# Output stores moved behind block 3's transposing DMAs, the order inside block 0's second product, and block 4's first product as a plain one

## The chip, the core and the metric

The kernel runs on one core of a Trainium2 chip. The metric is the device time of one execution in microseconds (us). Engines are named as in the profile: PE is TensorE (PEld its weight loads), DVE is VectorE, ACT is ScalarE, POOL is GpSimd, SP is SyncE, which issues nearly all DMAs of this kernel.

## The reference, cut to what matters

```python
# retention: q, k, v of shape (B=4, H=8, S=768, D=64)
for t in range(S):
    state = gamma * state + k_t v_t^T           # one 64x64 state per batch and head
    y[:, :, t] = scale * q_t state
# the rows of y, heads side by side: x is (3072, 512)
h = x @ w_in                                    # (512, 2048)
g = h * tanh(softplus(h))                       # Mish
out = g @ w_out                                 # (2048, 512), float32
```

## The kernel before, in words

**Blocks.** The 3072 rows are 24 chunks of 128. Block 0 holds four chunks, each of the blocks 1 to 10 two; `first[blk]` is the first chunk of a block (0, 4, 6, 8, 10, 12 and so on). A block goes through retention (scores `at`, masked to `am`, outer products `u_ps`, states `mid` and `sth`, result `y_ps`, copied to `xt`), then the first product with `w_in` and Mish (`g`), then the second product with `w_out` (`o_ps`, collected in `osb`, stored to `out`). The parts of neighbouring blocks are interleaved by hand; every engine, SP's DMA queue among them, takes its instructions in the order in which the kernel writes them.

**The first product** has two forms. `g1(blk, u)` makes 64 plain matmuls of 128x256 for a block of two chunks (u = 0 to 7, eight matmuls each). `mixed_in(blk, last)` makes half of the product with seven smaller products in place of eight (Strassen-Winograd, 56 matmuls of 128x128, line 853) and half plain (32 of 128x256, line 873). Blocks from `MIX` on take `mixed_in`; in the kernel before `MIX` is 4. The sums of `mixed_in` go through six tiles of the tag `hsum`, asked for in this order: `m1` and `m5` (ACT copies, line 883), `h11` (DVE, line 888), `u2` (ACT), `h12` and `h22` (DVE). The last matmuls of `mixed_in`, `mm(pa, a(1, 1), t[3])`, write on the bank that `h22` reads.

**The second product** is `first_out` for block 0 and `seven(blk, ...)` for the others, both with seven products in place of eight. `seven` calls hooks between its products: `retain(blk + 1, later)` with `ready(later)`, which makes scores and outer products of the block after the next, and a hook that casts, transposes and loads what comes later.

**Chunks on their way in.** `load` issues three DMAs (q, k, v, lines 156 to 162). `casts_qk` (lines 422 and 425) and `casts_v` (line 432) scale and cast on POOL. `turn_by_dma` (line 437) transposes a chunk's q and k with one DMA into `qkt`. POOL's casts in `seven` begin with a one-column copy `summed` (line 1264), which reads a tile that DVE has just made, and so begin at a set point of the second product.

**Stores.** `seven` and `first_out` append the finished `osb` tiles to the list `stores`; `store_due(u)` (line 234) issues those that are due, inside the `g1` loop of blocks 1 to 3 and at the head of blocks from `MIX` on. `osb` has a tag of its own with five buffers. A pool hands out the buffers of a tag in the order in which they were given back; a tile that takes a buffer waits for the last reader of the tile before, and the last reader of an `osb` is its store.

**Helpers that the steps name.** `next_two(g)` runs in `seven(3)` with g = 14 and in `seven(4)` with g = 16: it transposes chunks g and g+1 and loads up to chunk g+3. `get_ready(blk + 1)` runs in the `g1` loop of blocks 1 to 3 (`tight`). In `first_out`, `turn_two` transposes chunks 4 and 5 on PE (line 255) and copies them out of PSUM with ACT and DVE; `kept_sum` makes `u3` on DVE (line 688); `outer_two` writes `u_ps` (line 353), which `pair_state` reads on DVE (line 366); `present_two` makes half of y (line 381) in two tiles of the tag `at`, which has two buffers, and `y_two` the rest.

Of the kernel before, what the change touches and what calls it, by code (L numbers as in the profile page):

```python
# [16 lines left out]
def kernel(  # L17
# [9 lines left out]
    nc = tc.nc  # L27
# [91 lines left out]
    loaded, cast, qkts, ats, ams, states, mids, us, ys = {}, {}, {}, {}, {}, {}, {}, {}, {}  # L119
    xts, gts, wins, wouts, wtmps = {}, {}, {}, {}, {}  # L120
    gtiles, tmats, gsums = {}, [], []
    ONE, MIX, BACK = 3, 4, 6
    nload, ncast = [0], [0]
    stores, weight_left, wsums = [], [], []

# [510 lines left out]
    def g1(blk, u):  # L636
        nt = BLOCKS[blk] * C
        per = TB // nt
        h_ps = g1_bank(blk, u)
        for j in range(per):  # L640
            s, f = divmod(u * per + j, FPS)
            for bp in range(NBP):
                wide = 2 * C if u >= NFB - 6 else nt
                for at in range(0, nt, wide):
                    cols = slice(at, at + wide)
                    nc.tensor.matmul(  # L646
                        h_ps[:, j, cols], wins[s][f // 2][:, bp, f % 2 * P:(f % 2 + 1) * P],
                        xts[blk][:, bp, cols], start=(bp == 0 and at == 0), stop=(bp == NBP - 1),
                        skip_group_check=blk == 0)
        room = NFB * TB // (2 * nt)  # L650
        at0, lies = divmod(u * per, room)
        if lies == 0:
            gtiles[blk, at0] = gp.tile([P, room, nt], FP16, name="g", tag="g", bufs=3)
        gt = gtiles[blk, at0][:, lies:lies + per]
        nc.scalar.activation(gt, h_ps, AF.Mish, scale=inv_boost3)  # L655
        for j in range(per):
            gts[blk, u * per + j] = gt[:, j]
# [33 lines left out]
    def first_out(load_more, cast_qk, cast_v, turn_two, sums, weight):  # L691

        hf = d_model // 2
        banks = {(0, 0): pxps.tile([P, 2, hf], FP32, name="o_ps", tag="px")}
        for ij in ((0, 1), (1, 0), (1, 1)):
            banks[ij] = mmps.tile([P, 2, hf], FP32, name="o_ps", tag="mm")
        open_banks = set(banks)
        osb = [op.tile([P, d_model], FP32, name="osb", tag="osb") for _ in range(CPB)]

        def mm(ij, x, w, fs=range(FPS)):  # L700
            for f in fs:
                for t in range(2):
                    nc.tensor.matmul(  # L703
                        banks[ij][:, t], x(f)[:, t * P:(t + 1) * P], w(f), start=ij in open_banks,
                        stop=f == fs[-1], skip_group_check=True)
                    open_banks.discard(ij)

        def a(i, j):
            return lambda f: gts[0, 2 * j * FPS + f][:, i * 2 * P:(i + 1) * 2 * P]

        def b(i, j):
            return lambda f: wouts[2 * i][:, f, j * hf:(j + 1) * hf]

        def s(i):
            return lambda f: sums[i - 1][:, f]

        def t(i):
            return lambda f: tmats[(i - 1) // 2][:, (i - 1) % 2, f]

        def plain(i, j, n, fs=range(FPS)):  # L720
            mm((i, j), lambda f: gts[0, n * FPS + f][:, i * 2 * P:(i + 1) * 2 * P],
               lambda f: wouts[n][:, f, j * hf:(j + 1) * hf], fs)

        def done(i, j, plus=None):
            for n in range(2):
                dst, src = osb[2 * i + n][:, j * hf:(j + 1) * hf], banks[i, j][:, n]
                if plus is None:
                    nc.scalar.copy(dst, src)
                else:
                    nc.vector.tensor_tensor(dst, src, plus[:, n], op=ALU.add)  # L730

        mm((0, 0), a(0, 0), b(0, 0))
        m1 = kept_sum(banks[0, 0])
        mm((0, 1), s(1), t(1))
        m5 = kept_sum(banks[0, 1])
        load_more()
        cast_qk()
        plain(1, 1, 1)
        plain(0, 0, 1)
        weight(0, 2)  # L740
        mm((0, 0), a(0, 1), b(1, 0))
        mm((0, 1), s(4), b(1, 1))
        mm((1, 0), s(2), t(2))
        u2 = kept_sum(banks[1, 0], m1)
        weight(0, 1)
        cast_v()
        turn_two()
        cast_wout(3, True)
        plain(0, 1, 1)
        mm((1, 0), s(3), t(3))  # L750
        u3 = kept_sum(banks[1, 0], m1)
        u35 = op.tile([P, 2, hf], FP32, name="hsum", tag="hsum", bufs=6)
        nc.gpsimd.tensor_tensor(u35, u3, m5, op=ALU.add)
        pair_scores(2, 0)
        pair_scores(2, 1)
        turn_both(CPB + 2)
        mm((1, 0), a(1, 1), t(4))
        plain(1, 0, 1)
        for j in (1, 0):
            plain(0, j, 3, range(2))  # L760
        outer_two()
        plain(0, 1, 3, range(2, FPS))
        done(0, 1, u2)
        plain(0, 0, 3, range(2, FPS))
        done(0, 0)
        present_two()
        weight(1, 1)
        plain(1, 0, 3)
        y_two()
        done(1, 0, m1)  # L770
        plain(1, 1, 3)
        done(1, 1, u35)
        for n in range(CPB):
            stores.append((0, out_rows(0, n), osb[n]))
# [150 lines left out]
    def seven(blk, masks, hooks, last):  # L925
        n, hf = NFB // 2, d_model // 2
        px = pxps.tile([P, hf], FP32, name="o_ps", tag="px")
        pb = mmps.tile([P, hf], FP32, name="o_ps", tag="mm")
        osb = [op.tile([P, d_model], FP32, name="osb", tag="osb") for _ in range(2)]

        def a(i, j):
            return lambda f: gts[blk, j * n + f][:, i * P:(i + 1) * P]
# [261 lines left out]
    def outer_two():  # L1194
        u = u_banks()[1][:1]
        for a in range(2):
            pair_outer(2, u, a)
        pair_state(2, u, 0)
# [7 lines left out]
    def y_two():  # L1206
        y = pairs["y"]
        pair_present(2, y, True)
        for m in range(2):
            pair_past(2, y, m)  # L1210
        for m in range(2):
            pair_xt(2, y, m, m == 1)
# [15 lines left out]
    def next_chunk(g):  # L1228
        turn_next(g)
        load_to(g + 3)  # L1230

    def next_two(g):
        turn_next(g)
        load_to(g + 3)
        turn_next(g + 1)
        load_to(g + 4)

    def next_one(g):
# [22 lines left out]
    def cast_behind(blk, i):  # L1261
        g = first[blk] + (6 if blk == 1 else 8)
        if ncast[0] < min(g, NCK):
            nc.gpsimd.tensor_copy(summed, gsums[blk % 2][:, i, NFB // 2 - 1, P - 1:])  # L1264
            if blk == 1:
                for n in range(g - 2, g):
                    casts_qk(n)
                for n in range(g - 2, g):
                    casts_v(n)
                ncast[0] = g  # L1270
            elif blk + 1 >= BACK:
                cast_to(g - 2)
                casts_qk(g - 2)
                ncast[0] = g
            else:
                cast_to(min(g, nload[0]))

    def tight(blk):

# [1 line left out]

    def plan_of(blk):
        a = first[blk] + 4
        plan = {u: [] for u in (0, 1, 5)}
        if tight(blk):
            plan[5] = [(get_ready, blk + 1)]
        elif blk < MIX:
            plan[0] = [(settle, blk + 1), (mask_two, blk + 1), (leave, blk + 1)]
        if blk == 1:
            plan[0] += [(load_to, a + 2)]  # L1290
            plan[1] += [(begin_load, a + 2)]
        elif blk < ONE:
            plan[1] += [(next_chunk, a)]
        return plan

    first_block()
    for blk in range(1, len(BLOCKS)):
        last = blk + 1 == len(BLOCKS)
        plan = plan_of(blk)
        if blk >= BACK:  # L1300
            second_of(blk - 1)
        if blk >= MIX:
            store_due(NFB)
            mixed_in(blk, last)
        elif blk > 1:
            weight_left.extend(in_sums(blk - 2))
        for u in range(NFB // 2 if blk < MIX else 0):
            store_due(u)
            g1(blk, u)
            if u in ((6, 7) if tight(blk) else (5, 7)):  # L1310
                sums_a(blk, u // 7)
            for fn, *args in plan.get(u, ()):
                fn(*args)
            if weight_left:
                weight_left.pop(0)()
        hooks = [[], [], []]
        if not last:
            later = blk + 2 if ONE <= blk < len(BLOCKS) - 2 else None
            hooks = [[(retain, blk + 1, later)],
                     [(next_one, first[blk] + 6)] if blk + 1 >= BACK else  # L1320
                     [(next_two, first[blk] + 6)] if blk >= ONE else
                     [(turn_load, first[blk] + 4)] if blk == 1 else
                     [(next_chunk, first[blk] + 5), (turn_load, first[blk] + 6)],
                     [(finish, blk + 1)] if later is None else []]
        if tight(blk):
            hooks[2].append((leave, blk + 1))
        seven(blk, [(mask_two, blk + 1)] if tight(blk) else [], hooks, last)
# [31 lines left out]
```

## Time and profile before

| what | value |
|---|---|
| device time, median of 3 runs | 197.19 us (196.53, 197.19, 197.45) |
| the profiled execution | 196.68 us, its span 194.9 us |
| mean granted TensorE clock | 0.998 |
| PE busy | 188.6 us (97%), 3124 matmuls |
| DVE, ACT, POOL busy | 138.8 (71%), 104.4 (54%), 74.5 us (38%) |
| DMA | 38.78 MB, mean 199 GB/s |

Times inside the text are counted from the start of the span. "x8" is a count of instructions, "[0.59 <-DMA ...]" the idle time of the engine before a row and what ended it. A DMA's row shows how long SP was held by issuing it; its landing is later.

### The profile page before, as it was taken

Reading aid. Unit: us, or ns where it says so; the run is one execution under the profiler, and the core shown is the slowest. Engines: PE = TensorE matmul, PEld = TensorE weight load, DVE = VectorE, ACT = ScalarE, POOL = GpSimd, SP = SyncE. Lnnn points to the kernel's source line nnn. Section 1 sums busy time; section 2 is a strip of 40 time slices with the busy share of each in tenths; the row PEclk is TensorE's granted clock in tenths of the full one; section 3 lists DMA queues with packets and bytes.
Section 4 is the critical chain, followed back from the end, with each engine's and each line's share of the span. In section 5 each row is a group of like instructions: output and inputs, shape, how many; then the busy total and the mean of one; then the engine's idle time right before and its main releaser. Section 6 shows DMA issues by size and latency. Waiting matters only on the chain.

```text
span 194.9 us, 7190 instructions
## 1 busy us (share of the span) xinstructions
PE 188.6 (97%) x3124; PEld 162.1 (83%) x3124; DVE 138.8 (71%) x270; ACT 104.4 (54%) x194; POOL 74.5 (38%) x98
## 2 busy tenths in 40 slices
PE   7998999899999999999998999999999999999993
PEld 7756478787888888888997998998998988988993
DVE  0796559875867877967983985965885885885462
ACT  3375766244552552554483584484574763763850
POOL 5362000578507846662647605525625700000000
PEclk9999999999999999999999999999999999999999
DMA  5999999999999999999999999999895250300202
GB/s 173 304 310 348 367 385 364 289 306 215 131 257 261 177 236 213 206 194 194 247 233 197 227 182 290 202 213 255 98 241 106 52 148 3 111 0 26 89 29 81
DMA packets 84303, 38.78 MB, mean 199 GB/s; under 512 B 57776, under 2 KB 78896, under 8 KB 84272
## 3 DMA queue, kind: packets, MB, share of 16 engines
q1 hardware_dynamic: 84128, 38.28, 87.4%
q8 instruction: 24, 0.39, 0.9%
q10 hardware_dynamic: 144, 0.05, 0.2%
q14 instruction: 7, 0.06, 0.1%
HBM read 27.31 MB, written 6.29 MB: 172 GB/s over the span
## 4 chain that ended last, share of the span: by engine, by line
PE 51%; DMA 25%; SPq 12%; POOL 6%; DVE 2%; issue 1%; ACT 1%; POOLq 0%
PE o_ps L946 21%; PE h_ps L873 11%; DMA qf<-in_q_dram 10%; PE h_ps L853 10%; DMA vf<-in_v_dram 5%; DMA wi<-in_moe_w_in_dram 5%; SPq L284 4%; SPq L188 3%; PE o_ps L703 3%; DMA qkt<-qk 3%; PE h_ps L646 3%; SPq L162 2%; POOL v L432 2%; DMA kf<-in_k_dram 2%; SPq L437 2%; PE y_ps L559 2%
## 5 line engine op out<-in xcount | busy, mean ns | idle before, releaser
L646 PE MATMUL h_ps<-xt,win 128*128 128x256 f16 (+1 forms) x272 | 34.3, 285 | 0.0
L946 PEld LDWEIGHTS <-gsum 128*128 128x128 f16 x320 | 30.3, 98 | 3.8
L646 PEld LDWEIGHTS <-win 128*128 128x128 f16 x272 | 26.3, 98 | 6.6
L655 ACT ACTIVATE g<-h_ps 128x512 f16<-128x512 f32 x38 | 22.7, 597 | 15.2 <-PE h_ps L646 15.2
L946 PE MATMUL o_ps<-tmat,gsum 128*128 128x256 f16 x240 | 29.7, 273 | 0.0
L873 PE MATMUL h_ps<-xt,win 128*128 128x256 f16 x224 | 29.0, 273 | 0.0
L946 PEld LDWEIGHTS <-g 128*128 128x128 f16 x248 | 23.4, 98 | 2.6
L961 DVE TENSOR_TENSOR osb<-o_ps,snap 128x256 f32<-128x256 f32 (+1 forms) x33 | 13.8, 417 | 13.5 <-PE o_ps L946 9.6
L952 ACT COPY snap<-o_ps 128x256 f32<-128x256 f32 (+1 forms) x33 | 12.2, 369 | 20.1 <-PE o_ps L946 20.1
L873 PEld LDWEIGHTS <-win 128*128 128x128 f16 x224 | 20.7, 98 | 1.9
L864 ACT ACTIVATE g<-h_ps 128x512 f16<-128x512 f32 x35 | 19.9, 587 | 3.1 <-PE h_ps L873 3.1
L422 POOL TENSOR_TENSOR qk<-qf,qvs 128x512 f16<-128x512 f32 x18 | 19.4, 1076 | 4.3 <-DMA qf<-in_q_dram 4.3
L432 POOL TENSOR_TENSOR v<-vf,qvs 128x512 f16<-128x512 f32 x18 | 19.5, 1093 | 2.8 <-DMA vf<-in_v_dram 2.7
L883 ACT COPY hsum<-h_ps 128x512 f32<-128x512 f32 x21 | 12.3, 585 | 15.1 <-PE h_ps L853 14.9
L425 POOL TENSOR_TENSOR qk<-kf,qvs 128x512 f16<-128x512 f32 x18 | 18.8, 1042 | 4.2 <-DMA kf<-in_k_dram 4.0
L888 DVE TENSOR_TENSOR hsum<-h_ps,hsum 128x512 f32<-128x512 f32 x21 | 14.5, 691 | 7.4 <-PE h_ps L853 5.2
L946 PE MATMUL o_ps<-wout,g 128*128 128x256 f16 x160 | 19.1, 273 | 0.0
L608 ACT CAST xt<-y_ps 128x512 f16<-128x512 f32 x15 | 10.2, 735 | 11.1 <-PE y_ps L559 11.1
L853 PE MATMUL h_ps<-xt,wsum 128*128 128x128 f16 x224 | 15.9, 219 | 0.0
L1264 POOL COPY summed<-gsum 128x1 f16<-128x1 f16 x7 | 3.0, 422 | 33.3 <-DVE gsum L813 27.0
L853 PEld LDWEIGHTS <-wsum 128*128 128x128 f16 x224 | 14.0, 98 | 0.3
L864 ACT ACTIVATE g<-hsum 128x512 f16<-128x512 f32 x21 | 13.3, 631 | 1.5 <-DVE hsum L888 1.4
(112 smaller groups left out, 301.6 us busy)
## 6 DMA issues: line engine op xcount, KB each, us to landing
kf<-in_k_dram SPq DMA_DIRECT2D x24, 256.0 KB, 5.2
vf<-in_v_dram SPq DMA_DIRECT2D x24, 256.0 KB, 5.6
out_dram<-osb SPq DMA_DIRECT2D x22, 256.0 KB, 3.8
qf<-in_q_dram SPq DMA_DIRECT2D x20, 256.0 KB, 4.6
wi<-in_moe_w_in_dram SPq DMA_DIRECT2D x6, 512.0 KB, 8.8
wt<-in_moe_w_out_dram SPq DMA_DIRECT2D x2, 1024.0 KB, 10.3
wt<-in_moe_w_out_dram SPq DMA_DIRECT2D x4, 512.0 KB, 7.9
qfirst<-in_q_dram SPq DMA_DIRECT2D x2, 512.0 KB, 4.6
```

What stands on the lines that cost most here:

```text
L422: nc.gpsimd.tensor_tensor(in_place(q16.rearrange("p (w x) d -> p w x d", x=2)), by_head(qf), scale_by_head(qs_two[:, heads]), op=ALU.mult)
L425: nc.gpsimd.tensor_tensor(k16.rearrange("p (y w) d -> p w y d", y=2), kf.rearrange("p (w y) d -> p w y d", y=2), boosts.rearrange("p (w y) ...
L432: nc.gpsimd.tensor_tensor(cast[g][2], loaded.pop(g)[2], vs[g % 2].unsqueeze(2).broadcast_to((P, H, D)), op=ALU.mult)
L646: nc.tensor.matmul(h_ps[:, j, cols], wins[s][f // 2][:, bp, f % 2 * P:(f % 2 + 1) * P], xts[blk][:, bp, cols], start=(bp == 0 and at == 0) ...
L655: nc.scalar.activation(gt, h_ps, AF.Mish, scale=inv_boost3)
L853: nc.tensor.matmul(o_ps[:, f], w(f // 2, k)[:, f % 2 * P:(f % 2 + 1) * P], x[:, k], start=begin and f == 0 and k == 0, stop=k == 1, skip_g ...
L864: nc.scalar.activation(to, src, AF.Mish, scale=inv_boost3)
L873: nc.tensor.matmul(h_ps[:, f], wins[w][h // 2][:, k, h % 2 * P:(h % 2 + 1) * P], xts[blk][:, k, :2 * C], start=k == 0, stop=k == NBP - 1)
L883: nc.scalar.copy(m, o_ps)
L888: nc.vector.tensor_tensor(m, x, y, op=ALU.add)
L946: nc.tensor.matmul(o_ps[:, cols], x(f), w(f)[:, cols], start=first and z == 0, stop=z == n - 1, skip_group_check=True)
L961: nc.vector.tensor_tensor(dst, o_ps[:, cols], plus, op=ALU.add)
```

## The change: what it does

The stores leave the `g1` loop. `store(n)` issues the next n of the list: four (block 0's) in `next_two(14)`, behind the transposing DMAs of chunks 14 and 15 and around the loads of chunk 16; two (block 1's) at the head of block 4; four (block 2's and block 3's) in `next_two(16)`: two ahead of the transposing DMA of chunk 17, two behind the loads of chunk 18. As more of them are unstored at a time, the `osb` tiles of blocks 1 to 3 come from the tag `hsum`. `MIX` becomes 5, so block 4's first product is plain. In `first_out` eight plain matmuls go ahead of `turn_two`, `present_two` goes right behind `outer_two` with `y_two` earlier too, and one DVE sum moves into block 1. Block 1's `get_ready` goes one u later. POOL's casts of blocks 2 to 4 take q and k of both chunks first, then v. In block 0, u = 5 to 9 are made in columns of 256 instead of 512.

```diff
-    ONE, MIX, BACK = 3, 4, 6
+    ONE, MIX, BACK = 3, 5, 6
...
-                wide = 2 * C if u >= NFB - 6 else nt
+                wide = 2 * C if u >= 5 else nt
...
         cast_v()
+        plain(0, 1, 1)
         turn_two()
         cast_wout(3, True)
-        plain(0, 1, 1)
         mm((1, 0), s(3), t(3))
...
         outer_two()
+        present_two()
+        plain(1, 0, 3, range(2))
         plain(0, 1, 3, range(2, FPS))
         done(0, 1, u2)
         plain(0, 0, 3, range(2, FPS))
         done(0, 0)
-        present_two()
-        weight(1, 1)
-        plain(1, 0, 3)
         y_two()
+        weight(1, 0)
+        plain(1, 0, 3, range(2, FPS))
         done(1, 0, m1)
...
-        osb = [op.tile([P, d_model], FP32, name="osb", tag="osb") for _ in range(2)]
+        osb = [
+            op.tile([P, d_model], FP32, name="osb", tag="osb") if blk > ONE else
+            op.tile([P, d_model], FP32, name="osb", tag="hsum", bufs=6) for _ in range(2)]
...
+    def store(n):
+        for _ in range(n):
+            _, dst, osb = stores.pop(0)
+            nc.sync.dma_start(dst, osb)
+
     def next_two(g):
         turn_next(g)
-        load_to(g + 3)
-        turn_next(g + 1)
+        if g == first[ONE] + 6:
+            turn_next(g + 1)
+            store(2)
+            load_to(g + 3)
+        else:
+            store(2)
+            turn_next(g + 1)
+            load_to(g + 3)
+        store(2)
         load_to(g + 4)
...
-                cast_to(min(g, nload[0]))
+                both = range(ncast[0], min(g, nload[0]))
+                for n in both:
+                    casts_qk(n)
+                for n in both:
+                    casts_v(n)
+                ncast[0] = both.stop
...
-        plan = {u: [] for u in (0, 1, 5)}
+        ready_at = 6 if blk == 1 else 5
+        plan = {u: [] for u in (0, 1, ready_at)}
         if tight(blk):
-            plan[5] = [(get_ready, blk + 1)]
+            plan[ready_at] = [(get_ready, blk + 1)]
...
-        elif blk > 1:
+        elif blk in (2, 3):
             weight_left.extend(in_sums(blk - 2))
+        elif blk == MIX - 1:
+            store(2)
         for u in range(NFB // 2 if blk < MIX else 0):
-            store_due(u)
             g1(blk, u)
```

## The prediction

> **What bounds the kernel now.** I read the page first: PE is busy for 188.6 of 194.9 us, so what counts is PE's order and its few idle moments. I then asked for PE's own waits:
>
> ```profile
> PE at L480 <- DMA qkt<-qk: 0.6, 1, 0.6
> PE t_ps L255 <- POOL qk L305: 0.5, 1, 0.5
> PE o_ps L703 <- DVE hsum L688: 0.2, 1, 0.2
> ```
>
> From 16 us to the last matmul at 191.9 these are nearly all. The first is the one place where a DMA reaches PE: at 105.57, in block 4's second product, the transposed chunk 15. The chain of waits runs through that DMA back along SP, POOL's casts and the loads to 55.8, so the DMA queue has run just in time for 50 us. The stages of blocks 4 and 5, and the end:
>
> ```profile
> 93.78:108.64 14.86, 14.27 (x267) 12.86 (x264) 11.15 (x27) 8.64 (x16) 8.55 (x9) 1.00 1.08 226
> 108.64:122.95 14.31, 14.31 (x269) 13.02 (x267) 10.72 (x25) 8.51 (x16) 4.58 (x5) 1.00 1.25 234
> 192.00:194.90 2.90, 0.00 (x0) 0.00 (x0) 0.27 (x1) 0.00 (x0) 0.00 (x0) 0.88 0.32 102
> ```
>
> The columns are length, busy PE, PEld, DVE, ACT, POOL, granted clock, DMA share, GB/s. The DMA engines are full (1.08 and 1.25) in both stages. SP's timeline shows the queue pushing back; a transposing DMA's issue takes 1.24 at 149.38, when the queue is empty, and 3.68 here:
>
> ```profile
> 105.39 1.69 SPq L234 DMA_DIRECT2D out_dram<-osb  x2
> 107.18 2.21 SPq L437 DMA_TRANSPOSE qkt<-qk  x1
> 109.45 0.58 SPq L162 DMA_DIRECT2D qf<-in_q_dram  x1
> 110.08 0.53 SPq L162 DMA_DIRECT2D kf<-in_k_dram  x1
> 110.65 1.20 SPq L162 DMA_DIRECT2D vf<-in_v_dram  x1
> 111.96 3.68 SPq L437 DMA_TRANSPOSE qkt<-qk  x1
> ```
>
> These are block 3's stores, chunk 16's transpose, chunk 18's loads and chunk 17's transpose. The last lands 6.0 after its issue, at 117.9 (the tile's own view at that time).
>
> **Small parts on PE.**
>
> *Block 4's plain first product.* It removes 56 matmuls of 128x128 and 32 of 128x256 (6.69 us, 93.78 to 100.47) and adds 64 of 128x256. Blocks 2 and 3 run these at 0.1094 each (line 646, 48 in 5.25): 7.00. **+0.31**. The sums that go (seven DVE, three ACT) were beside PE; block 5's mask and states move into 7 us of `g1`, where DVE has room.
>
> *Columns of 256.* 20 matmuls of 512 (0.2158 start to start) become 40 of 256 (0.1092): **+0.05**.
>
> *Chunk 15's transpose.* Eight stores (blocks 0 to 2) that were issued before it go behind it; each takes the queue about 0.65 (two of 256 KB land 5.5 and 4.9 after issues 1.31 apart). It comes some 5 us earlier; the wait goes: **-0.59**. Next late on PE there is nothing else.
>
> *`first_out`.* The eight matmuls fill the 0.5 before `turn_two`, but all turns now run behind them and end 0.2 later (four of them ran before the wait). From there the chain is ACT's two copies (1.08), DVE's two (0.76) and `u3` (0.61), which PE awaited for 0.2 already; what was filled ahead is waited for there, and PE resumes 0.2 later than before. Then `present_two` comes right behind `outer_two`. Its second tile takes the buffer that DVE's `mid` reads:
>
> ```profile
> 45.26 0.42 DVE L366 TENSOR_TENSOR mid<-u_ps,sth 128x256 f16<-128x256 f32 x1 [0.98 <-PE u_ps L353]
> ```
>
> ```profile
> 44.78 0.44 PE L353 MATMUL u_ps<-v,qk 64*64 64x64 f16 x16
> 45.15 1.05 PE L703 MATMUL o_ps<-wout,g 128*128 128x256 f16 x8
> 46.13 0.25 PE L381 MATMUL y_ps<-am,v 64*64 64x128 f16 x4
> ```
>
> Eight matmuls from 45.15 to 46.13 covered `mid`, over at 45.68. Without them PE waits about 0.5. One change of matmul shape fewer gives back 0.1. **+0.6** (ends 0.2 and 0.9).
>
> *At nothing:* the DVE sum that moves (0.68) falls into DVE's idle 1.98 ahead of 54.79; `get_ready` one u later delays three states of 0.42, read 5 us later; POOL's new order brings the second k 1.04 sooner, and v, later by 2.1, is read after the transpose has landed. Uncovered, each costs its own length, all under 2.1.
>
> So PE comes to block 5's last product of `mixed_in` at 114.88 + 0.31 + 0.05 - 0.59 + 0.6 = 115.25.
>
> **The part that decides: `hsum`.** After the change all six `hsum` buffers hold the unstored `osb` of blocks 1 to 3. Block 5's `mixed_in` asks for six again; in the order of return `m1`, `m5` take block 1's, `h11`, `u2` block 2's, and **`h12`, `h22` block 3's**, whose stores are issued behind the transpose of chunk 17 and the loads of chunk 18. DVE takes its instructions in order: `h12` waits, and behind it `h22`, the states and the sums of `g`; PE then waits at `mm(pa, a(1, 1), t[3])` for `h22`. Before, block 5 ran:
>
> ```profile
> 112.00 0.69 DVE L888 TENSOR_TENSOR hsum<-h_ps,hsum 128x512 f32<-128x512 f32 x1
> 113.04 0.69 DVE L888 TENSOR_TENSOR hsum<-h_ps,hsum 128x512 f32<-128x512 f32 x1 [0.36 <-ACT hsum L883]
> 114.14 0.69 DVE L888 TENSOR_TENSOR hsum<-h_ps,hsum 128x512 f32<-128x512 f32 x1 [0.40 <-PE h_ps L853]
> ```
>
> ```profile
> 114.88 0.61 PE L853 MATMUL h_ps<-xt,win 128*128 128x128 f16 x8
> ```
>
> *When do the stores land?* Up to block 3's second store the new order has on SP just what the old one has up to chunk 17's transpose: ten stores, loads to chunk 18, transposes to 17. A full queue that works in order ends the same set at the same time: 117.9. It is later by what the queue idles. The transpose of chunk 14 can't be issued before its k is cast, which begins at a point of block 3's second product (cast over at 93.6, or 94.2 with PE 0.6 later), while the loads ahead, rid of six stores, land near 98.1 - 3.9 = 94.2: with the transpose's 3.1 from an empty queue, about 2 idle. I take 1 of the 2: 118.9. Block 1's and block 2's stores, a transpose and more ahead, land by about 113 and hold up little.
>
> *Then:* the first store is 0.65 ahead, `h12` 0.69, `h22` 0.69 behind the second, PE at 118.9 + 0.9 = 119.8. PE waits **4.55** (3.55 without idle queue, 5.55 with all of it). ACT has five Mish of 0.6 queued behind `h12`, which `seven(5)` reads: **+0.4** (0 to 0.6).
>
> *The clock.* Two rows show what idleness does: the first 46 matmuls of 128x128 take 5.09 us (107 ns each; 56 in block 5), and at the end the clock falls (0.88 over 2.9 us with PE at 0: a half for the last 0.7, so 2.2 us after the last matmul). A 4.5 us wait is longer than 2.2: the clock halves, and up to 5.1 us then run at half speed, which loses 0 to 2.55. I take **+1.5**. The Trainium skill (TensorE: Matmul & The Clock Gate, The HAM clock gate) states that the clock halves after a whole idle window of about 3.4 us, the windows running freely; by that a wait of 4.55 would hold a whole one in only a third of the cases. The row at the end, 2.2 us, speaks for less, and I go by the row.
>
> **Sum**, against the profiled execution's own 196.68 (1.78 outside its span; 0.51 below the median 197.19, so a median may come 0.5 higher): +0.37 by 115.25, +4.55, +0.4, +1.5 = +6.8: **203.5 us**.
>
> **Rivals.**
>
> *A: the queue keeps its lead, and PE never waits (not slower).* 196.68 + 0.37 = 197.05. It decides at the second store's landing: by 115.25 - 0.9 = 114.35. For it: in an empty queue k of 16 cast at 107, transposes issued in 1.24 each, stores in 0.4, loads in 0.6 and a landing of 2.3 (155.73) give about 114.8, close to the point. Against: shares of 1.08 and 1.25 and issues held 3.68; eight more stores lie in just this stretch. The same time comes if `h12` were not to take block 3's buffer, so that the change in `hsum` isn't what I read. 8%.
>
> *B: as A, and `first_out` gains.* If `mid` doesn't hold `present_two`, and both waits there (0.7) go: 196.68 + 0.36 - 0.59 - 0.7 = 195.75, over 0.5% faster by a hair. Against: the chain ACT, DVE, `u3` is untouched. 5%.
>
> *C: the wait is there, the clock stays.* 203.5 - 1.5 = 202.0 (a wait within whole windows, or shorter). With the stores at 116.5, if part of the lead is kept, 196.68 + 0.37 + 2.15 + 0.2 = 199.4. 27%.
>
> *D: forecast* with its bounds: 60%, from 201 (wait 3.55, clock 0.4) to 206.4 (wait 5.55, ACT 0.6, clock 2.55, and 0.6 more if `first_out` and queue are both at their worst).
>
> **Numbers.** 0.5% is 1.0 us, about what this measurement can tell from no change. Faster by more: B, 0.05. Within: A, 0.08. Slower: C and D, 0.87. The range runs from C's lower case, 199.4, to D's upper end, 206.4; outside lie A and B and little else.
>
> **What would show it.** In the changed profile: PE's longest wait is `h_ps` L853 on DVE `hsum` L888, 3.5 to 6 us, near 115 to 120; DVE's L888 waits there for DMA `out_dram<-osb`; the clock is below 1.00 in that slice or the next. PE `at` L480 no longer waits for `qkt`; PE L381 waits for DVE L366 near 45.5; block 1 starts 0.6 later; block 4's L646 takes 7.0. I am wrong if block 3's stores land before 114.3, or if `h12` starts without them.

## The result: 5.3% slower, by a wait that the prediction names and sizes too small, and by the clock behind it

The changed kernel takes 207.82 us (median of 207.43, 207.60, 207.82, 207.98 and 208.37; a sixth execution, disturbed, took 486.44 us and is left out), the kernel before 197.38 (median of 6). The ratio is 1.0531, 95% interval 1.0498 to 1.0564. The profiled execution took 207.82 us, its span 205.9 us, against 196.68 and 194.9: +11.1 where +6.8 was forecast: the direction is right, the size is outside the range (199.4 to 206.4 us).

PE's own waits in the changed kernel, the three longest behind the start of the program (total, times, longest; us):

```profile
PE h_ps L854 <- DVE hsum L889: 3.9, 1, 3.9
PE h_ps L854 <- ACT g L865: 2.4, 1, 2.4
...
PE y_ps L381 <- DVE mid L366: 0.5, 1, 0.5
```

The first and the third are as forecast (line 888 is now 889, 853 is 854); the second, and the size of what hangs on both, are not. The wait for `qkt` at L480 is gone. Block 5 in PE's timeline:

```profile
113.96 0.61 PE L854 MATMUL h_ps<-xt,win 128*128 128x128 f16 x8 [2.40 <-ACT g L865]
...
115.48 1.92 PE L874 MATMUL h_ps<-xt,win 128*128 128x256 f16 x8
...
123.22 1.01 PE L854 MATMUL h_ps<-xt,win 128*128 128x128 f16 x8 [3.91 <-DVE hsum L889]
```

Before, the last of these rows stood at 114.88 and took 0.61; eight matmuls of 128x256 took 1.04, not 1.92. So there are two waits, and half speed behind each. (A row of PE lasts to the modelled end of its last matmul; from start to start the eight of 128x256 took 1.71, before 0.87, and the eight of 128x128 0.81, before 0.45.) Who was waited for, in ACT's and then in DVE's timeline:

```profile
112.83 0.58 ACT L884 COPY hsum<-h_ps 128x512 f32<-128x512 f32 x1 [5.21 <-DMA out_dram<-osb]
```

```profile
121.88 1.29 DVE L889 TENSOR_TENSOR hsum<-h_ps,hsum 128x512 f32<-128x512 f32 x2 [6.15 <-DMA out_dram<-osb]
```

Both end on stores: `m1` on block 1's (landed 112.75), `h12` and `h22` on block 3's (landed 121.75 and 122.44). Block 1's were issued from 106.73 on, ahead of chunk 16's transpose. SP's timeline shows block 2's just ahead of chunk 17's transpose and block 3's behind it and the loads of chunk 18; this last pair held SP for 3.09:

```profile
111.72 1.08 SPq L1238 DMA_DIRECT2D out_dram<-osb  x2
112.91 1.44 SPq L437 DMA_TRANSPOSE qkt<-qk  x1
...
116.34 3.09 SPq L1238 DMA_DIRECT2D out_dram<-osb  x2
```

The windows of two us in and behind the first wait, and of block 5's `mixed_in` and `seven` (length, busy PE, PEld, DVE, ACT, POOL, granted clock, DMA share, GB/s):

```profile
112.00:114.00 2.00, 0.04 (x1) 0.03 (x1) 0.17 (x1) 1.17 (x3) 2.00 (x3) 1.00 1.22 185
...
116.00:118.00 2.00, 2.00 (x15) 1.63 (x14) 0.00 (x0) 0.79 (x2) 0.00 (x0) 0.50 1.02 243
...
108.76:124.03 15.27, 8.96 (x91) 7.77 (x89) 5.88 (x12) 4.61 (x9) 4.08 (x4) 0.82 1.10 263
124.03:133.79 9.76, 9.76 (x178) 7.77 (x177) 4.67 (x12) 3.62 (x8) 2.51 (x3) 0.76 0.69 161
```

The clock's records are at a half from 115.09 to 118.50 and from 121.92 to 128.74. Before, `mixed_in(5)` took 6.69 (now 15.27) and `seven(5)` 7.45 (now 9.76). From block 6 on the two executions run alike, the changed one 11.0 later. So the whole loss is block 5:

| step, at PE | forecast | measured |
|---|---|---|
| start of block 5 | +0.37 | +0.12 (108.76, before 108.64) |
| wait at the last product of `mixed_in(5)` | +4.55 | +8.22 (123.22 less 114.88 + 0.12) |
| that product and `seven(5)`: clock and ACT | +1.9 | +2.67 (0.81 - 0.45, 9.76 - 7.45) |
| start of block 6 | +6.82 | +11.01 |

### The profile page after: what moved, and what is told of

The parts are those of the page before. It is cut to its first block, busy times and chain, and to the rows that moved or that the text cites. A ratio compares the mean times of both kernels' runs of the same rounds, so it can differ in the third digit from the quotient of the medians.

```text
span 205.9 us, 7172 instructions
## 1 busy us (share of the span) xinstructions
PE 193.2 (94%) x3120; PEld 166.5 (81%) x3120; DVE 133.3 (65%) x263; ACT 102.5 (50%) x191; POOL 73.3 (36%) x98
## 4 chain that ended last, share of the span: by engine, by line
PE 82%; DMA 8%; DVE 2%; SPq 2%; ACT 1%; issue 1%; POOL 1%; DVEq 0%
PE o_ps L949 29%; PE h_ps L646 20%; PE h_ps L874 8%; PE h_ps L854 8%; PE o_ps L703 6%; DMA kf<-in_k_dram 3%; DMA out_dram<-osb 3%; PE y_ps L559 3%; DMA qfirst<-in_q_dram 2%; PE t_ps L255 1%; PE u_ps L487 1%; PE at L480 1%; SPq L162 1%; PE y_ps L381 1%; PE h_ps L628 1%
## 5 line engine op out<-in xcount | busy, mean ns | idle before, releaser
L646 PE MATMUL h_ps<-xt,win 128*128 128x256 f16 (+1 forms) x356 | 41.5, 276 | 0.0
L646 PEld LDWEIGHTS <-win 128*128 128x128 f16 x356 | 34.6, 98 | 5.4
L655 ACT ACTIVATE g<-h_ps 128x512 f16<-128x512 f32 x46 | 27.5, 597 | 19.8 <-PE h_ps L646 19.8
L949 PEld LDWEIGHTS <-g 128*128 128x128 f16 x248 | 24.2, 101 | 3.4
L874 PE MATMUL h_ps<-xt,win 128*128 128x256 f16 x192 | 26.0, 280 | 0.0
L889 DVE TENSOR_TENSOR hsum<-h_ps,hsum 128x512 f32<-128x512 f32 x18 | 12.4, 691 | 15.2 <-PE h_ps L854 7.0
L949 PE MATMUL o_ps<-wout,g 128*128 128x256 f16 x160 | 20.8, 287 | 0.0
L874 PEld LDWEIGHTS <-win 128*128 128x128 f16 x192 | 18.4, 101 | 2.0
L884 ACT COPY hsum<-h_ps 128x512 f32<-128x512 f32 x18 | 10.5, 586 | 16.6 <-PE h_ps L854 10.6
L865 ACT ACTIVATE g<-h_ps 128x512 f16<-128x512 f32 x30 | 17.1, 590 | 2.4 <-PE h_ps L874 2.4
L854 PE MATMUL h_ps<-xt,win 128*128 128x128 f16 x144 | 11.4, 224 | 6.3 <-DVE hsum L889 3.9
L854 PEld LDWEIGHTS <-win 128*128 128x128 f16 x144 | 9.8, 100 | 7.4 <-issue 6.7
L865 ACT ACTIVATE g<-hsum 128x512 f16<-128x512 f32 x18 | 11.3, 630 | 7.2 <-DVE hsum L889 7.2
```

The lines of the kernel that those rows point to most:

```text
L646: nc.tensor.matmul(h_ps[:, j, cols], wins[s][f // 2][:, bp, f % 2 * P:(f % 2 + 1) * P], xts[blk][:, bp, cols], start=(bp == 0 and at == 0) ...
L854: nc.tensor.matmul(o_ps[:, f], w(f // 2, k)[:, f % 2 * P:(f % 2 + 1) * P], x[:, k], start=begin and f == 0 and k == 0, stop=k == 1, skip_g ...
L865: nc.scalar.activation(to, src, AF.Mish, scale=inv_boost3)
L874: nc.tensor.matmul(h_ps[:, f], wins[w][h // 2][:, k, h % 2 * P:(h % 2 + 1) * P], xts[blk][:, k, :2 * C], start=k == 0, stop=k == NBP - 1)
L889: nc.vector.tensor_tensor(m, x, y, op=ALU.add)
L949: nc.tensor.matmul(o_ps[:, cols], x(f), w(f)[:, cols], start=first and z == 0, stop=z == n - 1, skip_group_check=True)
```

## Experiments

The theory: the shared tag `hsum` makes block 5's sums wait for late stores, and the clock falls in the waits. Rivals: the stores' new places by themselves (through late loads and transposes), block 4's plain product, and the order in block 0. All ratios are against the kernel before, run beside on the same chip.

**Nobody asks for the six tiles** (x_mix6).

```diff
-    ONE, MIX, BACK = 3, 5, 6
+    ONE, MIX, BACK = 3, 6, 6
...
-        elif blk == MIX - 1:
+        elif blk == 4:
             store(2)
+        elif blk == 5:
+            store_due(NFB)
```

> The changed kernel with MIX 6: block 5's first product is plain too, so that nothing asks for the six hsum tiles before block 6; the DMA order is kept (block 1's stores at the head of block 4, block 4's at the head of block 5). Theory (hsum: block 5's sums wait for buffers whose stores land at 112.8 to 122.4): PE has no wait over 0.5 us between 100 and 130, the granted clock stays full, and the time is that of the kernel before, 197.4, plus 0.54 (block 0) - 0.72 (block 4's second product) + 0.30 (block 4) + 0.3 (block 5's plain product): 197.8. Rival (the stores' new place itself, through late loads and transposes, whatever holds the buffers): 203 or more, with PE or the casts waiting for DMAs behind block 5.

197.72 us against 197.51, ratio 1.0019 (0.9998 to 1.0039): the 5% are gone with every store still at its new place. Block 3's stores even land as late as in the changed kernel, at 122.17 and 123.07. PE has no wait over 0.6 us behind the start of the program, and the clock stays full. The rival of the stores' new places by themselves falls, and with it block 4's plain product: here there are two of the kind.

**Block 0's stores back in block 1** (x_b0). As `store(n)` issues the next n of the list, every later store moves up by four with it; block 3's go to the head of block 4, ahead of chunk 16's transpose.

```diff
-        for _ in range(n):
+        for _ in range(min(n, len(stores))):
...
         for u in range(NFB // 2 if blk < MIX else 0):
+            if blk == 1:
+                store_due(u)
             g1(blk, u)
```

> The changed kernel with block 0's four stores back in block 1's first product; the rest of the list moves up by four: block 1's and block 2's stores then go behind the transposes of chunks 14 and 15, block 3's at the head of block 4, before the transpose of chunk 16. Theory: the queue works in 56 to 68 as it did before (DMA share 1.1 to 1.2 in place of 0.64 and 0.69), the transpose of chunk 8 still lands by 68, block 3's stores land by about 110, m1 (ACT) and h12 (DVE) find their buffers free, PE waits for neither, the clock stays full: 197.5. Rival (the loss comes from having more stores in front of block 4's and 5's chunks, or from the plain product and block 0): 202 or more.

197.42 us against 197.51, ratio 0.9997 (0.9979 to 1.0016). The forecast of the time held, its reason in part only: the DMA share in 56 to 62 came back (1.00, from 0.64), in 62 to 68 it did not (0.70). Block 3's stores landed at 111.97 and 112.62, later than the 110 expected and still in time for `h12`. What PE waits for now:

```profile
PE y_ps L381 <- DVE mid L366: 0.5, 1, 0.5
PE at L335 <- DVE qkt L261: 0.4, 1, 0.4
```

These are `first_out`'s; the new order in block 0 is in this kernel too, so the loss isn't there. Block 0's four stores at their old place, and the others up by four, undo the whole loss; which of the two does it, the next run takes apart.

**Block 0's stores back, all others where the change puts them** (x_b0only). This takes apart why block 3's stores were late.

```diff
             turn_next(g + 1)
-            store(2)
             load_to(g + 3)
...
             load_to(g + 3)
-        store(2)
+            store(2)
...
+            if blk == 1:
+                store_due(u)
             g1(blk, u)
```

> The changed kernel with block 0's stores back in block 1's first product, and every other store where the change puts it (block 1's at the head of block 4, block 2's ahead of chunk 17's transpose, block 3's behind the loads of chunk 18). It tests the term of the prediction that went wrong: block 3's second store at 117.9 plus the time that the queue idles. If the idle queue of 56 to 68 is what made it late by 4.5 (122.4), it lands now near 118 to 118.5, PE comes back near 119.3, and with some of the clock's loss the time is 201 to 203. Rival (the four stores just move the later ones up by their 2.6 us, and the order of the last ten DMAs, with chunk 17's transpose and six loads ahead, is what is late): it lands at 119.8, and the time is 203 to 205. Block 1's stores land before 110.5 and m1 does not wait.

204.41 us, ratio 1.0395 (1.0351 to 1.0439). `m1` waits no more. Block 3's stores landed at 118.52 and 119.21, between the two expectations. In PE's timeline:

```profile
119.99 0.98 PE L854 MATMUL h_ps<-xt,win 128*128 128x128 f16 x8 [4.79 <-DVE hsum L889]
```

This is the prediction's own picture: PE back at 119.99 (forecast 119.8), a wait of 4.79 (4.55), block 6 later by 6.76 (6.8: 129.54, before 122.78; the profiled execution is the fastest of four, whose median is 7.2 over the kernel before). What the changed kernel does beyond it comes from block 0's four stores. That they are late costs block 3's second store 3.2 us (122.44 less 119.21); four stores at 0.65 are 2.6, and the other 0.6 is not explained. Against the queue's old pace (117.9) 1.3 us are left, about what the prediction allowed for an idle queue at chunk 14's transpose (1 of 2). It does idle, one transpose later: chunk 15's is issued at 97.42, once POOL has cast its k, and the DMA share in 98 to 99 is 0.43 (0.20 in the changed kernel, 1.35 before). That this is the whole of the 1.3 isn't shown. Block 0's stores alone thus take the ratio from 1.0531 to 1.0395; what x_b0 gains beyond that comes from the others going up by four.

**Block 3's stores four DMAs sooner** (x_b3early).

```diff
         else:
-            store(2)
+            store(4)
             turn_next(g + 1)
             load_to(g + 3)
-        store(2)
+        if g == first[ONE] + 6:
+            store(2)
```

> The changed kernel with block 3's two stores issued together with block 2's, ahead of the transpose of chunk 17 and the loads of chunk 18. A dose: they should land about 4 to 5 us earlier, near 117.5, and so should h12, h22 and PE's return to the last product of block 5's first product (118.2 in place of 123.2). Theory (PE's end follows the second store's landing one to one, and the clock falls in both): about 203, between 201.5 and 204; the first wait, 2.4 us for m1 and block 1's stores, stays. Rival (the second wait is set by something else on the queue, such as chunk 17's transpose): no change, 207.9.

201.82 us, ratio 1.0226 (1.0177 to 1.0275). They landed at 117.03 and 117.98, and the second wait is gone altogether; the first is left:

```profile
PE h_ps L854 <- ACT g L865: 3.1, 1, 3.1
```

So the first wait, which in the changed kernel lies within the lateness of the second, costs by itself when the second goes. The time is as expected, the picture behind it is not: PE comes to the last product of `mixed_in(5)` at 121.24 and not at 118.2, held by the first wait and by the half clock behind it (113.96 to 120.78), and no longer by the landing of block 3's second store. That PE follows this landing one to one, as the theory had it, holds only while the landing comes last. The four executions had a mean granted clock of 0.983, 0.999, 0.991 and 1.000 and took 203.16, 200.89, 201.73 and 201.91 us.

**Keeping the clock up** (x_spin, then x_spin2). Unread matmuls on the free half of a tile of PSUM, in x_spin behind the last plain product's Mish, in x_spin2 (the edit shown) ahead of it.

```diff
-        ph = atps.tile([P, 2, 2, 2 * C], FP32, name="h_ps", tag="at")[:, 0]
-        plain(ph, 3 * n + 2)()
+        pht = atps.tile([P, 2, 2, 2 * C], FP32, name="h_ps", tag="at")
+        last_mish = plain(pht[:, 0], 3 * n + 2)
+        if blk == 5:
+            spin(64, 2, pht[:, 1].rearrange("p a (b c) -> p (a b) c", c=P).unsqueeze(1))
+        last_mish()
```

> The changed kernel with 32 more matmuls of 128x256 (3.5 us at the full clock) whose results nobody reads, on a free bank, just ahead of block 5's last product, where PE waits 3.9 us for DVE. They lie within the wait, so only the clock can change. Theory (the halved clock from 121.92 to 128.74 costs about 2.7 us behind the wait): 205.2, with a full clock from 123 on. If the clock is at a half as the matmuls begin, they take up to 7 us, outlast the wait by up to 3 and the time is 207 to 209. Rival (the clock's record costs nothing): 207.9.

214.03 us, ratio 1.0858 (1.0789 to 1.0928): slower by 6 than the changed kernel, which no theory expected. The matmuls wrote a tile that ACT was still to read, and waited for ACT, which waited for DVE, which waited for the stores:

```profile
PE h_ps L451 <- ACT g L865: 7.0, 1, 7.0
```

The run measures that new wait and says nothing of the price of the clock.

> The changed kernel with the same 32 unread matmuls of 128x256, now behind the last plain product of block 5 (it ends at 119.3) and ahead of that product's Mish, so that they wait for nobody: 119.3 to 122.8 at the full clock, inside the wait of 3.9 us that ends at 123.2. Only the clock can change, and ACT's Mish, which waits for DVE until 122.6 anyway. Theory: no half clock behind 121.9, 207.4 - 2.7 = 204.7. Rival (the clock's record costs nothing): 207.4. Second rival (a halved clock follows in a later window all the same): between 205 and 207.

206.52 us, ratio 1.0478 (1.0456 to 1.0501). PE's timeline, and the window of `seven(5)`:

```profile
119.48 3.66 PE L451 MATMUL h_ps<-ident 128*128 128x256 f16 x32
123.68 0.61 PE L854 MATMUL h_ps<-xt,win 128*128 128x128 f16 x8 [0.54 <-DVE hsum L889]
```

```profile
124.23:131.88 7.65, 7.62 (x178) 6.49 (x176) 4.86 (x13) 3.77 (x8) 2.51 (x3) 1.00 0.85 204
```

The half clock behind the first wait is there as before (115.27 to 118.69); from 118.69 on the clock stays full, `seven(5)` takes 7.65 in place of 9.76 and the product ahead of it 0.55 in place of 0.81: **in this stage the clock costs 2.4 us**. The time falls by 1.3 only, to where the second rival had it (205 to 207), but not for its reason, as no halved clock follows. In this execution block 3's second store lands 0.45 later (122.89), and PE stands once for 0.63 at 147.3 with nothing to wait for in the profile ("issue"). x_spin has the same stop at the same matmul (0.83 at 153.87) and the changed kernel has none there, so it seems to come with the added matmuls; why isn't shown.

**The small edits alone, on the kernel before** (p_first_out, p_turns, p_mix5).

```diff
 p_first_out: the new first_out, nothing else
 p_turns:
         turn_next(g)
-        load_to(g + 3)
         turn_next(g + 1)
+        load_to(g + 3)
         load_to(g + 4)
 (and q, k of both chunks cast ahead of v)
 p_mix5:
-    ONE, MIX, BACK = 3, 4, 6
+    ONE, MIX, BACK = 3, 5, 6
...
-        elif blk > 1:
+        elif blk in (2, 3):
```

> The kernel before with the new order inside block 0's second product alone. In the changed kernel block 1 started 0.54 us later. Theory: the same here, PE waiting about 0.5 for DVE's mid ahead of the first part of y, but of that 0.5 the wait of 0.59 at 105.57 for chunk 15's transpose, which the DMA queue sets, takes most back: 0 to +0.1, 197.4. Rival (the waits at the old place were the longer ones): block 1 starts no later.

> The kernel before with both transposes ahead of the loads in next_two, and POOL's casts of q and k of both chunks ahead of v. No store is moved. Theory: chunk 15's transpose comes about 3 us sooner, the wait of 0.59 at 105.57 goes, 196.8 (-0.6). Rival (loads of chunks 17 and 18 come late by what the transposes gain): the wait appears again at chunk 16 or 17, no gain or +0.5.

> The kernel before with MIX 5 alone: block 4's first product is plain. PE's part of block 4 is longer by 0.31; the wait of 0.59 for chunk 15's transpose behind it, which the DMA queue sets, shrinks by as much: +0 to +0.3, 197.4 to 197.7. Rival (the plain product is what the change loses by): +2 or more.

Against 197.96: 198.10, ratio 1.0008 (0.9979 to 1.0036); 197.57, 0.9981 (0.9950 to 1.0011); 197.49, 0.9975 (0.9947 to 1.0004). None is told from no change. That is what was expected of the first and the third. Of the second a gain of 0.6 was expected; in its profile the wait of 0.59 is gone, and PE waits 0.4 for `hsum` in block 5 (as it does in p_first_out's). With the plain product as well (p_both):

> The kernel before with block 4's first product plain and the transposes of chunks 14 to 17 ahead of the loads, nothing else. Theory: the plain product costs 0.31, the wait of 0.59 for chunk 15's transpose goes, and six sums of DVE and three copies of ACT less lie beside it: 197.0, 0.2% to 0.4% under the kernel before. Rival (no gain, the transposes' gain comes back as late loads): 197.4.

197.31 us against 197.30, ratio 1.0001 (0.9981 to 1.0022): no gain. DVE's sums of `xt` in block 5, in this version and then in the kernel before:

```profile
107.36 1.86 DVE L840 TENSOR_TENSOR xt<-xt 128x256 f16<-128x256 f16 x2
109.81 1.51 DVE L840 TENSOR_TENSOR xt<-xt 128x256 f16<-128x256 f16 x2
```

```profile
107.53 1.08 DVE L840 TENSOR_TENSOR xt<-xt 128x256 f16<-128x256 f16 x2
109.19 0.48 DVE L840 TENSOR_TENSOR xt<-xt 128x256 f16<-128x256 f16 x2
```

POOL's casts in p_both, and one of the kernel before:

```profile
108.03 1.04 POOL L425 TENSOR_TENSOR qk<-kf,qvs 128x512 f16<-128x512 f32 x1
109.03 2.14 POOL L432 TENSOR_TENSOR v<-vf,qvs 128x512 f16<-128x512 f32 x2
```

```profile
109.51 1.07 POOL L425 TENSOR_TENSOR qk<-kf,qvs 128x512 f16<-128x512 f32 x1 [1.38 <-DMA kf<-in_k_dram]
```

Before, POOL stood for 1.38 until k landed at 109.5, and DVE's second pair began in that pause. In p_both k is there earlier, and POOL casts without a pause from 108.03 to 111.17, just where DVE makes the four sums; they take 3.4 in place of 1.6, `h12` and `h22` come late, and PE waits 0.74 at 115.55. The wait for the transpose has turned into a wait for DVE. That POOL's casts are what slows DVE is read from these rows; no run takes the casts away.

**What the runs point to** (x_b0old: x_b0 with the old `first_out`; x_best: with block 0's old columns too).

> The version with block 0's stores back in block 1's first product (197.42, with 0.5 us of waiting for DVE's mid in block 0) and the old order inside block 0's second product, which starts block 1 0.54 us earlier. Theory: 196.9, 0.3% under the kernel before. Rival (the 0.54 comes back as a wait for a transpose, as in the kernel before): 197.4.

> What the other runs point to: the changed kernel with block 0's stores back in block 1's first product, the old order inside block 0's second product, and the old columns of 512 in block 0's first product. Theory: 0.05 under the version without the last edit, 196.8 against 197.3 of the kernel before, ratio 0.997 to 0.998. Rival: no difference from the kernel before, ratio 1.000.

196.86 against 197.30, ratio 0.9980 (0.9958 to 1.0002), and 196.85 against 197.56, ratio 0.9973 (0.9950 to 0.9997). The last beats both kernels, by an interval that only just leaves out no change; which of its parts does it isn't shown.

## Why the prediction was wrong, step by step

- **Block 4's plain product, +0.31:** `g1` took 6.99 in place of 6.69, +0.30. Right. **Columns, +0.05:** block 0's first product ended 0.05 later (31.54, 31.49). Right.
- **Chunk 15's transpose, -0.59:** it landed 4.8 earlier (100.72, before 105.53; forecast "some 5"), PE doesn't wait, and `seven(4)` took 7.45 for 8.17. Right; the 0.13 more is not explained.
- **`first_out`, +0.6:** PE waits 0.52 for `mid` at 45.82, and block 1 starts 0.54 later (49.47, 48.93), the columns' 0.05 among it. Right by its mechanism, 0.1 high.
- **The order in which `hsum` comes back:** right for both pairs that were waited for, block 1's for `m1`, block 3's for `h12` and `h22`. x_mix6 shows that this is the cause.
- **Block 1's stores "land by about 113 and hold up little":** the landing of block 1's was right (112.75), the conclusion wrong. ACT had been idle since 107.6, `m1`'s product was done at 109.4, and PE stood for 2.40. Block 2's landed at 114.91 and 115.60, later than forecast, and ACT waited 0.78 for the second (`u2`). The step was never worked out against the time at which `m1` is asked for. In the changed kernel it lies within the lateness of the second wait; in x_b3early it is what is left.
- **The step that failed, "I take 1 of the 2: 118.9":** block 3's second store landed at 122.44, 3.5 later. The prediction let the queue gain 3.9 us on the old order and lose only 1 to 2 at chunk 14's transpose. It lost the gain much earlier. With block 0's stores gone, SP had nothing to issue in block 1; in SP's timeline:

```profile
55.29 1.46 SPq L162 DMA_DIRECT2D qf<-in_q_dram  x1
62.22 3.62 SPq L437 DMA_TRANSPOSE qkt<-qk  x2
```

  The transpose of chunk 8 waits for POOL's casts, and those for a point of PE's second product. The windows of the changed kernel, then of the kernel before:

```profile
56.00:62.00 6.00, 6.00 (x134) 5.22 (x123) 5.13 (x10) 2.09 (x5) 2.32 (x3) 1.00 0.64 122
62.00:68.00 6.00, 6.00 (x94) 5.17 (x80) 4.76 (x9) 2.83 (x6) 5.38 (x6) 1.00 0.69 108
```

```profile
56.00:62.00 6.00, 6.00 (x92) 5.13 (x90) 4.64 (x11) 2.31 (x5) 2.51 (x3) 1.00 1.14 283
62.00:68.00 6.00, 6.00 (x70) 5.25 (x69) 5.10 (x9) 3.36 (x6) 5.41 (x5) 1.00 1.22 178
```

  Shares of 0.64 and 0.69 (before 1.14 and 1.22): the four stores used to be served there, beside a gate, at no cost. Taken out, they shorten next to nothing. The last load ahead of the gate lands at 60.91 (before 65.96), and then the queue stands: the transpose of chunk 8 lands at 66.60 (67.50). In x_b0only, with the four stores in their old place, it lands at 66.61. The two stores of block 1 that are gone too (issued at 69.98 and 76.38 before) fare alike: the queue is 2.61 ahead at chunk 12's transpose (86.08, before 88.69), chunk 13's waits for the cast of its k, over at 85.17, and lands only 0.53 ahead (88.89, before 89.42). The loads that were to "land near 94.2" land at 97.35 (before 98.10), 0.75 ahead and not 3.9. Put back in, where they land from 102.31 to 108.92, block 0's stores push every later DMA. x_b0only shows the size: 3.2 of the 3.5. "A full queue ends the same set at the same time" is not contradicted by any run; that the queue would be full wasn't looked up over the 50 us in which the set is issued.
- **The wait, 4.55:** PE came back at 123.22 in place of 119.8. With block 0's stores put back (x_b0only) the forecast's 4.55 is 4.79.
- **The clock, +1.5:** right by its mechanism, and mis-sized: 2.4 (x_spin2), near the upper bound of 2.55. **ACT's catch-up, +0.4:** `seven(5)` takes 7.65 at the full clock, 0.20 over the kernel before, within its bounds.

The miss of 4.2 us (11.01 against 6.82) is thus 3.67 of the wait, 0.77 of clock and ACT, less 0.25 that PE came sooner. Rival C lost by this too: the clock did fall, in each of the five executions (means of 0.975 to 0.983).

## What to carry to other kernels

In this kernel a DMA that was taken out of the queue saved time only as far as what followed it could be issued at once; look at each gate behind it (here a cast that hangs on PE's progress) before its length is counted as a gain, and look at the queue's busy share over the whole stretch, not at the place where it matters in the end. When tiles that wait to be stored share a tag with tiles that are needed soon, write for each request the landing of the store that frees it beside the time of the request, for the first request as for the last. And a wait on PE can have a second price, the clock behind it: here waits of 2.4 us and more had it in most executions, and a shorter or longer half clock by where they fell.

## What the runs showed of the hardware that was not expected

**The clock fell after a wait of 2.40 us.** In the changed kernel PE stood from 111.56 to 113.96, and the clock was at a half from 115.09 to 118.50, 3.41 us. The Trainium skill (TensorE: Matmul & The Clock Gate, The HAM clock gate) states windows of about 3.4 us that run freely, which agrees with the length, and a fall after a whole idle window, which does not: a wait of 2.40 can't hold one, so here a window that was idle for the most part was enough.

x_spin has nearly the same wait at another phase. Up to PE's last matmuls its clock is at a half from 122.17 to 129.00 only; counted back from there in steps of 3.41, windows end at 111.93 and 115.34, and the wait lies across the first edge. PE runs at full speed behind it:

```profile
113.88 0.61 PE L854 MATMUL h_ps<-xt,win 128*128 128x128 f16 x8 [2.28 <-ACT g L865]
...
115.21 1.04 PE L874 MATMUL h_ps<-xt,win 128*128 128x256 f16 x8
```

Counted by such windows, 2.17 us idle (x_b3early), 2.28 (the changed kernel) and 2.45 (x_spin2) out of 3.41 were followed by half speed; 1.95 (x_spin) and 1.45 (x_b0only, 113.24 to 116.65) were not. At half speed less is enough to stay there: in the changed kernel the window from 121.92 to 125.33 was idle for 1.30, and the next one ran at half speed too; in x_b3early 0.91 did the same. These are single profiles, with modelled ends of matmuls. That the windows run freely fits x_b3early, whose executions show mean clocks from 0.983 to 1.000 for one program (one window at half speed is 0.5 x 3.41 of 201, 0.0085), and x_b0only, with 0.992 once (203.57 us) and 0.983 three times (204.32, 204.50 and 206.01).

**DVE's sums of two tiles in SBUF took longer beside POOL's casts.** A pair of 128x256 takes 0.48 us while POOL is idle and 1.51 to 1.86 beside its casts of 1.04. The Trainium skill (SBUF — State Buffer, Who interferes with whom) states that a DVE instruction with two inputs in SBUF contends with a GpSimd instruction that reads SBUF, and that the pair of ports they share is an exclusive lock. p_both agrees with it.
